# Half of one weight ahead in float32, input tiles of 128 rows, more half output tiles: an attention and soft-MoE kernel on one core

## The chip, the core and the metric

The kernel runs on one core of a Trainium2 chip. TensorE (PE; PEld is its weight load), VectorE (DVE), ScalarE (ACT), GpSimd (POOL) and SyncE (SP) run side by side, and 16 DMA engines move data between HBM and the core's on-chip memory. POOL and SP issue the DMAs; a DMA that POOL issues can cast float32 to bf16 on the way, one that SP issues here copies as it is. The metric is device time in microseconds, the median of several runs.

## The reference

Attention comes first. There are 4 batches, 8 heads, 768 positions and a head dimension of 64. Heads 0, 2 and 6 see all earlier positions; the other five see the first 4 positions and a window of 64. The output is laid out as x, 3072 rows of 512. Then comes a soft mixture of experts with 32 slots, 4 for each of 8 experts:

```python
logits = x @ phi                              # phi: 512 x 32
d = softmax(logits, axis=0)                   # over the 3072 tokens
slot_input = (d.T @ x).reshape(8, 4, 512)
for e in range(8):
    slot_out[e] = relu(slot_input[e] @ w1[e]) @ w2[e]   # w1: 512 x 1024, w2: 1024 x 512
c = softmax(logits, axis=1)                   # over the 32 slots
out = c @ slot_out.reshape(32, 512)           # 3072 x 512
```

The inputs q, k, v are 18.9 MB in float32, w1 and w2 together 33.6 MB; the output is 6.3 MB.

## The kernel before

**A planner sets the order.** `Plan` (L33) holds operations with a name, the engines that may run them, a modelled duration, a due time (`key`), dependencies and buffers. `run` (L69) places them one after the other on a model of the engines and returns the order in which they are emitted; each engine then works through its own instructions in that order. `SHIFTS` (L167) is a table of numbers, one for each operation before the last phase: each moves a due time and may fix a copy to ACT or DVE.

**Loads.** POOL issues all loads of q, k, v and nearly all of the weights, with the cast to bf16, in one fixed order (`dma`, L330). A load is issued only when the eighth before it has landed (L331) and when its buffer is free. There are 11 buffers ("S8"). Batch 0 comes in half tiles (L352), 96 rows each. Batches 1 to 3 come as one tile of 96 partitions for each of q, k and v: 9 loads. The order is batch 0, w0, q1 k1 v1, w1, w2, q2 k2 v2, w3 to w5, q3 k3 v3, w6 to w10. The last weights go into memory that other tensors leave (L862 to L877): w11 to w13 whole, w14 and w15 in halves of 256 output columns, in the order 14 left, 15 left, 14 right, 15 right. (w0 to w7 are w1 of the eight experts, w8 to w15 their w2.)

**The front.** SP issues four DMAs at the start (L460): a quarter of w0 as float32, 4 KB for each of 128 partitions, into memory that is later `expT`; the flags of the heads, repeated for 128 partitions (8 KB in 128 packets); and phi in two DMAs, whose rows are pieces of 32 floats (512 packets). The other three quarters of w0 come through POOL's queue with the cast (L394). At 28 us POOL casts the float32 quarter in two operations (L525). DVE works out the flags on all partitions (L427), and from them ACT and POOL make head flags (L434) and DVE the masks (L440). PE meanwhile multiplies zeros, in groups ZF and ZG (L490 to L508), as fillers.

**Attention.** Each tile of q, k or v is turned by PE transposes (L577), 16 at a time into one of two PSUM buffers ("TR"), and evacuated by ACT or DVE (L321, L323). For each of 16 pairs of heads (p), five groups of score products (L610, `PGROUPS` at L197) go through ACT's exponential (L679) into `pt`; three DVE multiplications apply masks (L626). The score block of key block 0 and query block 5 is made separately, four pairs at once, in `ptx` (L691 to L711), and needs no mask of the diagonal. Products with v (L740) follow, are normalised on DVE (L761) and turned (L773). At the end of each batch come logits (L790), exponentials, slot sums (L821) and `expT` (L854).

**The experts and the output.** After the last batch: slot inputs (L892), fillers Z (L902), first layer H (L915), relu (L925), transposes (L937), second layer W2 (L953). W2.14.0 and W2.15.0 are the left halves of the last two experts' weights, W2.14.1 and W2.15.1 the right ones. After W2.15.0 PE makes the row sums RW (L980), DVE their reciprocals (L986), and ACT scales the left half of the slot outputs (SO.0, L992). Then come output tiles of 128 rows (OM, L1009; evacuation OE on ACT or DVE, L1017 and L1019). `NL = 3` groups of four tiles are made in halves: the left halves, columns 0 to 255, before W2.15.1, stored by POOL; the right halves after it, stored by SP; the other 12 tiles whole, stored by SP in three DMAs (L1025 to L1047).

```python
    ri_src = bass.AP(tensor=is_retrieval.tensor.reshape([H]).bitcast(I32), offset=0, ap=[[0, P], [1, 2 * H]])
    nc.sync.dma_start(w0f, moe_w1[0].rearrange("(di x) f -> di (x f)", x=4)[:, 0:2 * KB])
    a = pl.op("RW", on("PE", 0.7, 0.27), kt + 24, deps=[eto[b] for b in range(B)] + [o_st, w2o[0]], acq=[rw], emit=emit_rw,
```

Of the kernel before, what the change touches and what calls it, by code (L numbers as in the profile page):

```python
# [16 lines left out]
KB = 512  # L17
# [144 lines left out]
def act(cols, extra=0.0):  # L162
# [4 lines left out]
SHIFTS = [-192, 84, -330, 309, -90, -87, 300, -18, 120, -42, -48, -360, -132, -240, 42, -360, 57, -222, 12,  # L167
# [48 lines left out]
def kernel(  # L216
# [46 lines left out]
    phf = sb.tile([P, 4, NS], F32, name="phf")  # L263
# [9 lines left out]
    ri = sb.tile([P, 2 * H], I32, name="ri")  # L273
# [11 lines left out]
    w0f = expT.rearrange("p a c -> p (a c)")[:, 0:4 * KB].bitcast(F32)  # L285
# [4 lines left out]
    rne = xT.rearrange("p a c -> p (a c)")[:, 1792:1824].bitcast(F32)  # L290
# [39 lines left out]
    def dma(name, nbytes, buf, dst, src, deps=()):  # L330
        if len(chain) >= 8:  # L331
            deps = list(deps) + [chain[-8]]
        iss = pl.op("issue " + name, on("POOL", 0.645, 1.4), -100, deps=list(deps) + [fifo[0]],
                    acq=[buf] if buf else [], lead=1.3, emit=lambda o: nc.gpsimd.dma_start(dst(), src))  # L334
        fifo[0] = iss
        took = nbytes / 425000.0
        chain.append(pl.op("land " + name, {"DMA": (took, took + 1.3 + min(2.1, 0.22 * len(chain)))}, -100, deps=[iss] + chain[-1:], lead=3.4))
        return chain[-1]

    def raw_view(buf, p0, p1):  # L340
# [27 lines left out]
    def w_mem(i):  # L368

        m = late_mem[i]() if i in late_mem else slots[wbuf[i].slot][:, :]  # L370
        if i == 0:
            return m[:, 0:8 * KB].rearrange("p (h x) -> p h x", h=2)
# [726 lines left out]
```

## Time and profile before

| what | value |
|---|---|
| median of 3 runs | 150.85 us (150.83 to 151.16) |
| the profiled execution | 150.66 us |
| its span, first to last instruction | 148.9 us |
| granted TensorE clock, mean | 0.959 |
| instructions | 5316 |
| HBM read, written | 52.50 MB, 6.29 MB |

The profile's page gives busy times of each engine, the span in 40 slices with the share and the pace of the DMA engines, and the chain of work that ended last. The views of stretches give, for a window in microseconds, the busy time of PE, PEld, DVE, ACT and POOL (with the number of instructions in brackets), the granted clock, the mean DMA share and the GB/s written. A timeline row gives start, length, engine, line, operation, output and inputs, count, and in brackets the idle time before it and what ended it. A group row gives busy time and mean ns of one after the first bar, and idle time before it after the second.

### The profile page before, as it was taken

To read this page: it belongs to the slowest core of one execution; us is meant where nothing else is said; L and a number is where in the kernel's file an instruction comes from. 1 tells how busy PE (TensorE), PEld (TensorE's weight loads), DVE (VectorE), ACT (ScalarE), POOL (GpSimd) and SP (SyncE) were. 2 spreads that over 40 slices of the span, in tenths; PEclk is the share of its full clock that TensorE was granted. 3 is DMA by queue.
4 is the path that set the end of the run, shared out by engine and by line. 5 is a ranking of instruction groups with operands and counts; after the bars stand their busy time and mean duration, and the time that the engine had idled before them with its cause. 6 is when DMAs were issued, how large, how long until landed. Compare 5 with 4: busy or idle time off the path is not lost.

```text
span 148.9 us, 5316 instructions
## 1 busy us (share of the span) xinstructions
PE 124.9 (84%) x2351; PEld 85.2 (57%) x2351; DVE 109.0 (73%) x231; ACT 108.3 (73%) x139; POOL 34.2 (23%) x60
## 2 busy tenths in 40 slices
PE   6759999889999999998999999999959897659100
PEld 1256667568677676676766776756645553433000
DVE  1843699996999899999799999998974311749400
ACT  3134799989999978998799999999962450638300
POOL 6948411610201200310101104130170000520000
PEclk9999999999999999999999999999999999996855
DMA  5999999999999999999999999999999999999994
GB/s 116 162 209 211 227 205 216 216 214 216 210 217 215 216 216 212 212 218 214 215 214 214 216 214 217 216 212 215 216 215 212 203 198 198 166 328 308 390 425 207
DMA packets 14279, 33.18 MB, mean 223 GB/s; under 512 B 1392, under 2 KB 7024, under 8 KB 13872
## 3 DMA queue, kind: packets, MB, share of 16 engines
q0 software_dynamic: 11408, 27.53, 94.3%
q1 hardware_dynamic: 2848, 5.32, 10.0%
q8 instruction: 18, 0.29, 0.7%
q14 instruction: 5, 0.04, 0.1%
HBM read 52.50 MB, written 6.29 MB: 395 GB/s over the span
## 4 chain that ended last, share of the span: by engine, by line
PE 45%; DMA 20%; DVE 17%; ACT 7%; issue 4%; POOL 1%; DVEq 0%; ACTq 0%; POOLq 0%
DMA qk<-in_moe_w_dram 14%; PE pv L740 12%; PE sc L610 11%; PE tr L577 10%; ACT pt L679 6%; DMA slot<-in_q_dram 5%; DVE xv L761 4%; DVE pt L626 4%; PE bk L1009 3%; PE tr L773 3%; DVE vx L323 2%; PE tr L643 2%; DVE vf L658 2%; PE pv L504 2%; DVE slot L1019 1%
## 5 line engine op out<-in xcount | busy, mean ns | idle before, releaser
L679 ACT ACTIVATE pt<-sc 128x1024 bf16<-128x1024 f32 x80 | 76.8, 1042 | 6.0 <-PE sc L610 5.7
L610 PE MATMUL sc<-qk 64*128 64x128 bf16 (+3 forms) x288 | 32.5, 295 | 1.2 <-ACT pt L679 0.4
L626 DVE TENSOR_TENSOR pt<-pt,msk 128x1024 bf16<-128x1024 bf16 (+1 forms) x48 | 30.7, 658 | 2.1 <-ACT pt L679 1.8
L740 PEld LDWEIGHTS <-pt 128*128 128x128 bf16 x640 | 23.5, 97 | 8.6 <-issue 5.8
L740 PE MATMUL pv<-vx,pt 128*128 128x65 bf16 x352 | 26.3, 193 | 1.1 <-DVE xv L761 0.6
L577 PEld LDWEIGHTS <-slot 96*64 96x64 bf16 x768 | 20.4, 116 | 9.1 <-issue 5.8
L740 PE MATMUL pv<-vf,pt 128*128 128x65 bf16 x288 | 21.6, 194 | 1.0 <-DVE xv L761 0.9
L577 PE MATMUL tr<-ident,slot 96*64 96x96 bf16 x576 | 17.1, 208 | 0.5 <-DVE qk L323 0.5
L610 PEld LDWEIGHTS <-qk 64*128 64x128 bf16 x288 | 11.9, 94 | 8.6 <-issue 2.4
L323 DVE COPY qk<-tr 128x768 bf16<-128x768 bf16 x23 | 12.3, 551 | 6.2 <-PE tr L577 6.2
L761 DVE TENSOR_TENSOR xv<-pv,rs 128x768 bf16<-128x768 f32 (+1 forms) x17 | 15.5, 910 | 0.6
L334 POOL DMA_DIRECT2D slot<-in_moe_w_dram x11 | 7.6, 695 | 31.8 <-PE tr L577 26.7
L321 ACT COPY qk<-tr 128x768 bf16<-128x768 bf16 x9 | 7.2, 810 | 5.8 <-PE tr L577 5.7
L1017 ACT ACTIVATE slot<-bk,rrow 128x256 f32<-128x256 f32 (+1 forms) x17 | 8.1, 553 | 4.2 <-PE bk L1009 4.2
L1019 DVE TENSOR_SCALAR slot<-bk,rrow 128x256 f32<-128x256 f32 (+1 forms) x19 | 9.3, 560 | 0.6 <-PE bk L1009 0.5
L773 PE MATMUL tr<-ident,xv 128*128 128x128 bf16 x96 | 8.4, 220 | 1.3 <-issue 0.5
L577 PE MATMUL tr<-ident_u,slot 96*64 96x96 bf16 x192 | 7.7, 245 | 1.5 <-DMA slot<-in_q_dram 1.5
L323 DVE COPY xv<-tr 128x768 bf16<-128x768 bf16 x15 | 8.0, 552 | 0.8 <-PE tr L577 0.8
L1009 PE MATMUL bk<-msk,expT 128*128 128x256 bf16 (+1 forms) x36 | 7.8, 365 | 0.9 <-DVE msk L994 0.7
L323 DVE COPY vx<-tr 128x768 bf16<-128x768 bf16 x15 | 8.2, 549 | 0.0
L323 DVE COPY xT<-tr 128x768 bf16<-128x768 bf16 (+1 forms) x14 | 7.3, 524 | 1.1 <-PE tr L773 1.0
L643 PE MATMUL tr<-ident,xv 128*128 128x128 bf16 x96 | 8.1, 220 | 0.0
(102 smaller groups left out, 146.8 us busy)
## 6 DMA issues: line engine op xcount, KB each, us to landing
slot<-in_moe_w_dram POOLq DMA_DIRECT2D x10, 1024.0 KB, 25.2
out_dram<-slot SPq DMA_DIRECT2D x3, 1024.0 KB, 6.8
slot<-in_q_dram POOLq DMA_DIRECT2D x3, 768.0 KB, 30.2
slot<-in_k_dram POOLq DMA_DIRECT2D x3, 768.0 KB, 32.0
slot<-in_v_dram POOLq DMA_DIRECT2D x3, 768.0 KB, 22.7
out_dram<-slot SPq DMA_DIRECT2D x3, 512.0 KB, 3.8
qk<-in_moe_w_dram POOLq DMA_DIRECT2D x1, 1024.0 KB, 19.2
vx<-in_moe_w_dram POOLq DMA_DIRECT2D x1, 1024.0 KB, 22.2
```

Source lines behind the costliest of these rows:

```text
L323: nc.vector.tensor_copy(dst, src)
L577: nc.tensor.transpose(dst_, rv[:, i, 8 * c + s, :], idv)
L610: nc.tensor.matmul(scb[sc.slot][:, i, c:c + 128 * nb], kk, qq.rearrange("p b c -> p (b c)"), start=True, stop=True)
L626: nc.vector.tensor_tensor(pT, pT, mh, op=ALU.mult)
L643: nc.tensor.transpose(t[:, 128 * j:128 * (j + 1)], vT[:, 6 * n + j, :], ident)
L679: nc.scalar.activation(pTs[PTb[b, n].slot][:, :, 512 * g:512 * (g + 1)], scb[sc.slot], ACT.Exp, scale=scale)
L740: nc.tensor.matmul(pvb[:, h, 65 * i:65 * (i + 1)], lt, rhs, start=(j == 0), stop=(j == i))
L761: nc.vector.tensor_tensor(xo, pvw[:, :, :, 0:64], r.rearrange("p i (j o) -> p i j o", o=1).to_broadcast([P, 2, i1 - i0, 64]), op=ALU.mult)
L773: nc.tensor.transpose(t[:, 128 * i:128 * (i + 1)], xv[:, i, 128 * n:128 * (n + 1)], ident)
L1009: nc.tensor.matmul(banks[bf.slot][:, 0:w], out_lhs(gi, r), slot_out[:, cs], start=True, stop=True)
L1017: nc.scalar.activation(d, banks[bf.slot][:, 0:w], ACT.Copy, scale=sc_)
L1019: nc.vector.tensor_scalar(d, banks[bf.slot][:, 0:w], sc_, None, op0=ALU.mult)
```

## The change

- **w0**: SP brings half of it, 8 KB for each partition, as float32 into the memory of the second q/k buffer (`qk_mem[1]`), which batch 1 uses. POOL's load of w0 shrinks to the other half, 1 MB in HBM. POOL casts in four operations with due times 8 to 17 us; the evacuations of q and k of batch 1 wait for them.
- **Phi**: one DMA of 128 rows of 512 bytes, then a cast, four transposes, a copy, four transposes and a copy bring it into its layout. **Flags**: one packet to one partition; DVE, a PE product with ones, and DVE spread them.
- **Tiles**: q, k, v of batches 1 to 3 become seven tiles (six of 128 partitions, one of 96), loaded in 13 parts; one evacuation for each part. The loads' order is w0, tiles 0 and 1, w1, tile 2, w2, tiles 3 and 4, w3 to w5, tiles 5 and 6, w6 on.
- **Score groups**: block (0, 5) goes into the last group and block (1, 5) into the fourth; (5, 5) goes into `ptx` and gets a mask of its own, MX. The last group's mask covers 256 columns of each head instead of 384.
- **Fillers**: four ZG groups instead of eight; Z has 10 products of 448 columns instead of 17 of 256.
- **The end**: RW has an earlier due time and no longer waits for W2. `NL = 14` counts tiles: 14 in halves, 10 whole. The first right store is split in two.
- `SHIFTS` is a new table, and the planner's model lets the first load start at 4.6 instead of 3.4.

```diff
 PGROUPS = [
     [(0, 0, 4)],
     [(1, 1, 4)],
     [(2, 2, 4)],
-    [(3, 3, 3), (0, 4, 1)],
-    [(4, 4, 2), (5, 5, 1), (1, 5, 1)],
+    [(3, 3, 3), (1, 5, 1)],
+    [(4, 4, 2), (0, 4, 2)],
 ]
+TILES = [
+    [("q", 1, 0, 24), ("k", 1, 0, 8)],
+    [("k", 1, 8, 24), ("v", 1, 0, 16)],
+    [("v", 1, 16, 24), ("q", 2, 0, 24)],
+    [("k", 2, 0, 24), ("v", 2, 0, 8)],
+    [("v", 2, 8, 24), ("q", 3, 0, 16)],
+    [("q", 3, 16, 24), ("k", 3, 0, 24)],
+    [("v", 3, 0, 24)],
+]
+TKEYS = [10.8, 16.0, 31.0, 36.0, 50.0, 60.5, 68.4]
...
-    w0f = expT.rearrange("p a c -> p (a c)")[:, 0:4 * KB].bitcast(F32)
+    w0f = qk_mem[1][:, 0:8 * KB].bitcast(F32)
...
-    ri_src = bass.AP(tensor=is_retrieval.tensor.reshape([H]).bitcast(I32), offset=0, ap=[[0, P], [1, 2 * H]])
+    ri_src = bass.AP(tensor=is_retrieval.tensor.reshape([H]).bitcast(I32), offset=0, ap=[[2 * H, 1], [1, 2 * H]])
 
     def sp_front(o):
-        nc.sync.dma_start(w0f, moe_w1[0].rearrange("(di x) f -> di (x f)", x=4)[:, 0:2 * KB])
+        nc.sync.dma_start(w0f, moe_w1[0].rearrange("(di h x) f -> h di (x f)", h=2, x=2)[0])
         nc.sync.dma_start(ri, ri_src)
-        pv_ = moe_phi.rearrange("(i n d) s -> i d n s", i=2, n=4)
-        for i in range(2):
-            nc.sync.dma_start(phf[64 * i:64 * (i + 1)], pv_[i])
+        nc.sync.dma_start(phf, moe_phi.rearrange("(p a) s -> p (a s)", a=4))
...
-    for x in range(8):
+    for x in range(4):
         o_z = pl.op(f"ZG{x}", pe(52, 4), 105.0, deps=[o_z], lead=7.8 + 0.7 * x, emit=emit_zg, mode="full", mm=4)
...
-    o_fl = pl.op("flags", on("DVE", 1.55), -10, deps=[o_sp, o_kp], lead=7.0, emit=flags)
+    flb = Buf("TR")
+    o_fr = pl.op("flag row", on("DVE", 0.2), -10, deps=[o_sp], emit=flag_row)
+    o_fp = pl.op("flag product", on("PE", 0.07, 0.27), -10, deps=[o_fr, o_tab], acq=[flb], mode="r32", mm=1,
+                 emit=lambda o: nc.tensor.matmul(trb[flb.slot][:, 0:H], unit[:, 0:128], frow, start=True, stop=True))
+    o_fl = pl.op("flags", on("DVE", 0.45), -10, deps=[o_fp, o_kp], rel=[flb], emit=flags)
...
-    o_phi = pl.op("phi", on("DVE", 0.15), T * 1.5, deps=[o_sp], lead=15.0, emit=lambda o: nc.vector.tensor_copy(phi, phf))
+    o_p = pl.op("phi cast", on("DVE", 0.2), T * 2.0, deps=[o_sp], lead=7.0, emit=lambda o: nc.vector.tensor_copy(phw, phf))
+    o_p = pl.op("phi T1", pe(56, 4), T * 2.1, deps=[o_p, o_id], acq=[pb1], emit=phi_t1, mode="c32", mm=4)
+    o_p = pl.op("phi E1", copy_engs(512), T * 2.2, deps=[o_p], rel=[pb1], emit=phi_e1)
+    o_p = pl.op("phi T2", pe(40, 4), T * 2.3, deps=[o_p], acq=[pb2], emit=phi_t2, mode="r32", mm=4)
+    o_phi = pl.op("phi E2", on("DVE", 0.15), T * 2.4, deps=[o_p], rel=[pb2],
+                  emit=lambda o: nc.vector.tensor_copy(phw, tr_bf(pb2.slot, 4 * NS)))
...
-    o_w0 = [pl.op(f"w0 cast {x}", on("POOL", 1.2), 27.0, deps=[o_sp, wland[0]], lead=26.5 + 1.5 * x,
+    o_w0 = [pl.op(f"w0 cast {x}", on("POOL", 1.2), 8.0 + 3 * x, deps=[o_sp, wland[0].deps[0]], lead=8.0 + 2 * x,
...
+    def tile_transposes(ti):
+        parts = TILES[ti]
+        R = 4 * sum(x1 - x0 for _, _, x0, x1 in parts)
...
+                for s in range(8):
+                    for i in range(2):
+                        nc.tensor.transpose(t[64 * i:64 * (i + 1), :, s, :], rv[:, i, 8 * c + s, :], ident[0:R, 0:R])
...
+            for x, b, x0, x1 in parts:
+                def emit_e(o, c=c, tr=tr, x=x, b=b, x0=x0, x1=x1, y0=y0):
+                    copy(o, dst_of(x, b)()[:, x0:x1, 32 * c:32 * (c + 1)],
+                         tr_bf(tr.slot, 8 * R).rearrange("p (x y) -> p x y", y=32)[:, y0:y0 + x1 - x0, :])
...
+            def emit_mx(o, b=b, ns=ns):
+                px = ptx[PTXb[b].slot][:, :, ns[0]:ns[-1] + 1, :]
+                mh = msk.rearrange("p (i n) c -> p i n c", i=2)[:, :, ns[0]:ns[-1] + 1, 256:384]
+                nc.vector.tensor_tensor(px, px, mh, op=ALU.mult)
...
-    a = pl.op("RW", on("PE", 0.7, 0.27), kt + 24, deps=[eto[b] for b in range(B)] + [o_st, w2o[0]], acq=[rw], emit=emit_rw,
+    a = pl.op("RW", on("PE", 0.7, 0.27), kt + 14, deps=[eto[b] for b in range(B)] + [o_st], acq=[rw], emit=emit_rw,
...
-    NL = 3
...
+    NL = 14
+    halved = [(gi, min(4, NL - 4 * gi)) for gi in range((NL + 3) // 4)]
...
+        for r0, r1 in [(0, 2), (2, 4)] if gi == 0 else [(0, n)]:
+            store("SP", "r", gi, r0, r1, slice(256, 512), kt + 41 + gi + 0.1 * r0)
```

More of the change, by code (lines that the diff above doesn't have):

```diff
@@ L336, in dma @@
         took = nbytes / 425000.0
-        chain.append(pl.op("land " + name, {"DMA": (took, took + 1.3 + min(2.1, 0.22 * len(chain)))}, -100, deps=[iss] + chain[-1:], lead=3.4))
+        chain.append(pl.op("land " + name, {"DMA": (took, took + 1.3 + min(2.1, 0.22 * len(chain)))}, -100, deps=[iss] + chain[-1:], lead=4.6))
         return chain[-1]
@@ L528, with phi_t1, phi_e1, phi_t2 @@
-    batch_loads(1)
+    pb1, pb2 = Buf("TR"), Buf("TR")
+    phw = phi.rearrange("p n s -> p (n s)")
+    def phi_t1(o):
+        t = tr_bf(pb1.slot, DM)[0:NS]
+        for a in range(4):
+            nc.tensor.transpose(t[:, P * a:P * (a + 1)], phw[:, NS * a:NS * (a + 1)], ident)
+    def phi_e1(o):
+        copy(o, t1.rearrange("s (n i y a) -> s n i y a", n=4, i=2, a=4),
+             tr_bf(pb1.slot, DM)[0:NS].rearrange("s (a i n y) -> s n i y a", a=4, i=2, n=4))
+    def phi_t2(o):
+        for n in range(4):
+            nc.tensor.transpose(tr_bf(pb2.slot, 4 * NS)[:, NS * n:NS * (n + 1)], t1[:, 128 * n:128 * (n + 1)],
+                                ident[0:NS, 0:NS])
@@ L529 @@
+    load_tile(0)
+    load_tile(1)
     load_w(1)
+    load_tile(2)
     load_w(2)
-    batch_loads(2)
+    load_tile(3)
+    load_tile(4)
     for i in (3, 4, 5):
         load_w(i)
-    batch_loads(3)
+    load_tile(5)
+    load_tile(6)
     for i in range(6, 11):
@@ L549, in dst_of, with transposes @@
         return {"q": lambda: qTs[QTb[b].slot], "k": lambda: kTs[KTb[b].slot], "v": lambda: vT}[x]
-    def transposes(x, b):
-        raw = raws[x, b]
-        tb = {"q": QTb, "k": KTb, "v": VTb}[x][b]
-        dst = dst_of(x, b)
-        first = True
-        for part in ((0, 1) if b == 0 else (None,)):
+    def transposes(x):
+        raw, tb, dst, first = raws[x, 0], {"q": QTb, "k": KTb, "v": VTb}[x][0], dst_of(x, 0), True
+        for part in (0, 1):
             es = []
-            for c in range(2 if b == 0 else 4):
+            for c in range(2):
@@ L593, in transposes @@
-                es.append(pl.op(f"E{x}{b}.{part or 0}.{c}", copy_engs(768), key, deps=[a], rel=[tr], emit=emit_e))
-                first = False
-            if b == 0:
-                ev[x, 0, part] = es
-            else:
-                ev[x, b] = es
+                            nc.tensor.transpose(t[64 * i:64 * (i + 1), :, :, s, :], rv[:, i, 8 * c + s, :], ident_u)
+                a = pl.op(f"T{x}0.{part}.{c}", pe(23, 16), key, deps=[lands[x, 0, part], o_iu, tb.op],
+                          acq=[tr] + ([tb] if first else []), rel=[raw], emit=emit_t, mode="c64", mm=16)
@@ L600, in evs @@
     def evs(x, b, n):
-        return ev[x, 0, n // 2] if b == 0 else ev[x, b]
+        return ev[x, 0, n // 2] if b == 0 else [e for x0, x1, e in ev[x, b] if x0 < 6 * n + 6 and x1 > 6 * n]
     def sc_mms(sc, b, parts):
@@ L624, in f @@
             else:
-                pT, mh = pT[:, :, 2048:2432], mh[:, :, 256:640]
+                pT, mh = pT[:, :, 2048:2304], mh[:, :, 256:512]
             nc.vector.tensor_tensor(pT, pT, mh, op=ALU.mult)
         return f
-    for b in range(B):
-        for x in "qkv":
-            transposes(x, b)
+    for x in "qkv":
+        transposes(x)
+    for ti in range(len(TILES)):
+        tile_transposes(ti)
     for b in range(B):
```

139 lines of the change are left out of this document (72 added, 67 removed), and 57 rows, old and new, of the table SHIFTS.

## The prediction

> **What bounds the kernel now.** I read the slices of the page first, then the stretches, then the chain of work that ended last, then the timeline of the end.
>
> ```profile
> PE 124.9 (84%) x2351; PEld 85.2 (57%) x2351; DVE 109.0 (73%) x231; ACT 108.3 (73%) x139; POOL 34.2 (23%) x60
> ...
> DMA  5999999999999999999999999999999999999994
> GB/s 116 162 209 211 227 205 216 216 214 216 210 217 215 216 216 212 212 218 214 215 214 214 216 214 217 216 212 215 216 215 212 203 198 198 166 328 308 390 425 207
> ```
>
> No compute engine fills the span, but the DMA line is full from the second slice to the last but one. GB/s counts written bytes: a load that casts float32 to bf16 writes half of what it reads, so 215 here and 425 at the end (float32 stores) are the same pace.
>
> ```profile
> 0.00:2.00 2.00, 0.85 (x3) 0.41 (x4) 0.24 (x1) 1.27 (x1) 0.88 (x5) 1.00 0.06 14
> 2.00:4.00 2.00, 1.57 (x5) 0.33 (x3) 0.76 (x1) 0.01 (x1) 1.92 (x6) 1.00 1.00 223
> 4.00:6.00 2.00, 1.46 (x5) 0.56 (x6) 1.50 (x12) 0.59 (x2) 2.00 (x7) 1.00 0.92 135
> 6.00:8.00 2.00, 1.49 (x4) 0.30 (x2) 1.83 (x7) 0.00 (x0) 2.00 (x5) 1.00 1.15 202
> ...
> 50.00:60.00 10.00, 9.52 (x234) 7.20 (x227) 9.41 (x19) 8.69 (x11) 0.50 (x1) 1.00 1.06 215
> ```
> ```profile
> 20.00:31.00 11.00, 10.27 (x202) 7.26 (x201) 10.60 (x23) 10.85 (x12) 3.61 (x5) 1.00 1.06 214
> ```
> ```profile
> 20.00:108.00 88.00, 84.33 (x1818) 61.60 (x1815) 81.40 (x159) 83.94 (x98) 15.01 (x21) 1.00 1.06 214
> ```
>
> The columns are PE, PEld, DVE, ACT and POOL busy time, then clock, DMA share and GB/s. From 20 us on the loads run at 214, whatever the engines do. Only the front falls short. Beside the loads PE, DVE and ACT are busy 84.3, 81.4 and 83.9 of 88 us: a second bound, close behind.
>
> ```profile
> 109.84 21.38 DMA qk<-in_moe_w_dram
> 131.26 0.42 PE bk L953 x8
> ```
> ```profile
> 125.87 0.40 PE L953 MATMUL bk<-qk,xT 128*32 128x256 bf16 x8 [0.86 <-DMA qk<-in_moe_w_dram]
> ...
> 126.20 0.75 PE L980 MATMUL bk<-cols,expT 128*128 128x1 bf16 x24
> 126.32 0.47 ACT L992 ACTIVATE msk<-bk,rcs 128x256 bf16<-128x256 f32 x1 [4.13 <-PE bk L953]
> ...
> 126.85 0.93 PE L1009 MATMUL bk<-msk,expT 128*128 128x256 bf16 x7
> 126.99 0.31 DVE L986 RECIPROCAL rrow<-bk 128x24 f32<-128x24 f32 x1 [3.31 <-PE bk L980]
> 127.39 2.30 ACT L1017 ACTIVATE slot<-bk,rrow 128x256 f32<-128x256 f32 x6 [0.59 <-PE bk L1009]
> ...
> 132.32 5.80 PE L1009 MATMUL bk<-msk,expT 128*128 128x256 bf16 x24 [0.66 <-DVE msk L994]
> 132.72 6.85 DVE L1019 TENSOR_SCALAR slot<-bk,rrow 128x256 f32<-128x256 f32 x13 [0.45 <-PE bk L1009]
> ```
> ```profile
> 131.50:134.50 3.00, 2.34 (x22) 1.48 (x15) 2.27 (x6) 1.75 (x5) 0.00 (x0) 0.80 0.99 341
> 134.50:135.00 0.50, 0.50 (x3) 0.22 (x2) 0.50 (x2) 0.49 (x2) 0.00 (x0) 0.50 0.26 82
> 135.00:139.00 4.00, 3.12 (x11) 1.02 (x9) 4.00 (x8) 3.47 (x6) 0.00 (x0) 0.78 1.00 340
> 140.00:147.00 7.00, 0.00 (x0) 0.00 (x0) 0.00 (x0) 0.00 (x0) 0.00 (x0) 0.51 1.00 419
> ```
>
> The last weight is used at 131.26. After that the end is a queue of stores: half tiles at 341 and 340, whole tiles at 419, with one hole at 134.5. The output is 6.29 MB, so the end moves with two things: when the loads let go of the DMA engines, and when the first left half is ready. The second starts at W2.15.0 (125.87), which waits for a load, but only 0.86 us of it.
>
> **The front.** These are the four kinds of transfer that the change touches (queue, KB of one, us from issue to landing).
>
> ```profile
> slot<-in_q_dram POOLq DMA_DIRECT2D x2, 384.0 KB, 8.5
> ...
> expT<-in_moe_w_dram SPq DMA_DIRECT2D x1, 512.0 KB, 4.5
> ...
> phf<-in_moe_phi_dram SPq DMA_DIRECT2D x2, 32.0 KB, 9.1
> ri<-in_is_retrieval_dram SPq DMA_DIRECT2D x1, 8.0 KB, 4.2
> ```
>
> From 0 to 6 us the engines wrote 2 x (14 + 223 + 135) = 744 KB. Of these 524 KB are w0's float32 rows and 8 KB the flags, read once; the other 212 KB are cast, so read as 424. That is 0.96 MB read. At 430 GB/s (2 x 215) from 2.0 us on it would be 1.72 MB: a hole of 0.76 MB, or 1.8 us. SP's w0 rows are there 4.5 us after their issue, POOL's first q only after 8.5. The change puts another 524 KB there and takes it from POOL's w0 load: 524 / 430 = 1.2 us if all of it falls into the hole, 0 if none does. Phi in 128 packets instead of 512 and the flags in one instead of 128 free slots from 6 us on: the row of 6 to 8 lacks 13 GB/s, some 0.1 us, and the row of 4 to 6 lacks more for the same reason in part; I take 0.3. Loads end **1.5 us earlier**, bounds 0.1 to 1.9.
>
> The first q rows go behind more bytes of SP, but ahead of fewer phi packets. If the hole takes SP's rows, they land as now; if not, 1.2 us later. I take 0. The flags now wait for one packet behind w0's rows, then a DVE operation, a PE product and DVE again. Behind them DVE has the head masks and a copy, PE the fillers and the first transposes:
>
> ```profile
> 9.03 1.49 PE L577 MATMUL tr<-ident_u,slot 96*64 96x96 bf16 x32 [1.54 <-DMA slot<-in_q_dram]
> ...
> 12.66 0.85 PE L577 MATMUL tr<-ident_u,slot 96*64 96x96 bf16 x16
> ```
> ```profile
> 13.63 0.56 DVE L323 COPY qk<-tr 128x768 bf16<-128x768 bf16 x1 [4.46 <-PE tr L577]
> ```
>
> PE idles 1.54 us ahead of 9.03, DVE 4.46 us ahead of 13.63: the detour costs nothing unless the flags come over 2 us later. Phi's eight transposes and two copies go into the same slack. Four fewer filler groups could leave PE at its early pace (0.85 us for 16 transposes; 0.53 later) for longer: 0 to 1.3 us for 64 transposes, taken at 0, since the real ones run back to back from 15 us.
>
> ```profile
> 33.31 0.53 PE L577 MATMUL tr<-ident,slot 96*64 96x96 bf16 x16 [0.45 <-DVE qk L323]
> ```
>
> **Casts of w0 on POOL.** There are four instead of two, at 8 to 16 us instead of 28. On POOL the loads of the first tiles and the flag copies queue behind them. POOL has by then issued seven loads, 5.8 MB, which is 13 us of the stream from 5 us on, so a delay of some 4 us starves nothing.
>
> ```profile
> 27.97 1.81 POOL L526 CAST slot<-expT 128x512 bf16<-128x512 f32 x2
> ```
> ```profile
> 27.42 0.82 DVE L658 TENSOR_TENSOR vf<-vx,fmx 128x528 bf16<-128x528 bf16 x1
> ```
> ```profile
> 48.70 0.43 DVE L658 TENSOR_TENSOR vf<-vx,fmx 128x528 bf16<-128x528 bf16 x1
> ```
>
> Beside the cast, the same DVE product took 0.82 instead of 0.43 us. Two more contacts at 0.39 are 0.8 us of DVE, but in its slack of the front: 0, up to 0.8. The Trainium skill, "SBUF — State Buffer", § Who interferes with whom, says that a VectorE instruction with two SBUF inputs and a GpSimd instruction that reads SBUF exclude each other for the whole instruction. By it a contact may cost a whole cast; the trace agrees that there is a price, at less than half of that.
>
> **Tiles of 128 rows.** Nine loads of 96 rows become thirteen parts of seven tiles. The stretch of 20 to 31 us is q1, k1 and v1 in 96 rows at 214; 50 to 60 is weights in 128 rows at 215. So the shape gains nothing on the DMA. The Trainium skill's SBUF page, § Summary: rules for kernel authors, would have 128 partitions for a DMA-bound transfer; by it 96 rows might run at three quarters, 161, and the nine loads (14.2 MB read, 33 us at 430) would win 11 us. The trace excludes that. At most eight loads are in flight; any eight in a row of the new ones still read over 7 MB, 17 us, so the stream has work.
>
> On the engines:
>
> ```profile
> L626 DVE TENSOR_TENSOR pt<-pt,msk 128x1024 bf16<-128x1024 bf16 x32 | 22.0, 699 | 1.1 <-ACT pt L679 0.8
> ...
> L577 PE MATMUL tr<-ident,slot 96*64 96x96 bf16 x576 | 17.1, 208 | 0.5 <-DVE qk L323 0.5
> ...
> L323 DVE COPY qk<-tr 128x768 bf16<-128x768 bf16 x23 | 12.3, 551 | 6.2 <-PE tr L577 6.2
> ...
> L626 DVE TENSOR_TENSOR pt<-pt,msk 128x768 bf16<-128x768 bf16 x16 | 9.1, 576 | 1.0 <-ACT pt L679 1.0
> ...
> L323 DVE COPY xT<-tr 128x384 bf16<-128x384 bf16 x2 | 0.7, 352 | 0.4 <-PE tr L773 0.4
> ```
>
> Transposes fall from 576 to 448, each a third longer: equal columns, 128 weight loads fewer, perhaps 1 us of PE. Evacuations rise from 36 to 52 for the same columns. Two copies (768 in 551 ns, 384 in 352) give 153 ns for each extra one: 16 x 0.153 = 2.4 us on DVE and ACT together. The third mask shrinks from 768 to 512 elements: 699 - 576 = 123 ns for 256 elements, 16 times, 2.0 us saved. The new mask of the last diagonal block costs 0.7 for three batches and two halves for the first, some 2.9. Together +3.3 us on two engines, 1.6 us of each, against 4 to 7 us of idle time that each has in 88. The score groups lose a part (six products instead of four now), 32 products of PE. A new table of shifts orders all this anew; no row prices an order, and ACT's 4.1 us of idle bound it both ways. I take the end of compute as **unmoved**, bounds -1 to +2.5.
>
> **The end.** The row sums (0.75 us of PE at 126.20) move ahead. The left product at 126.85 waited for ACT's slot sums (126.79) anyway, but its evacuation began 0.54 later, where on the right side 0.40 is enough: -0.15 (0 to -0.5). Two more left tiles and the split first right store fill the hole at 134.5: (341 - 82) x 0.5 / 341 = 0.38, I take -0.35. Halves go at 340 instead of 419: two tiles are 0.52 MB, 1.54 instead of 1.25 us, +0.3. Loads that end before the left stores begin collide less with them: -0.1.
>
> **Sum.** W2.15.0 comes 0.86 us earlier, no more, since PE is then the later one (loads alone would give 1.5). -0.86 - 0.15 - 0.35 + 0.3 - 0.1 = -1.16. The profiled execution took 150.66 us around its span of 148.9, so 149.5; the median of the runs is 150.85, 0.19 above, so **149.7**.
>
> **Rivals.**
>
> *Compute comes earlier too.* PE loses 128 weight loads and 32 products, and the order is new. With compute 1 us earlier W2.15.0 is bounded by the loads: -1.5 instead of -0.86, so 149.0; with the whole hole filled 148.6. For it: all three engines are busy 93 to 96%, so each saved operation may count. Against: DVE and ACT get more work.
>
> *The hole isn't free.* SP's rows ran at 223 GB/s or less, not 430; the extra ones would hold the same engines until 7 us. First q lands 1.2 us later, compute with it, loads gain 0.5: W2.15.0 at +0.34, the end at about 0, 150.9. This is also the case in which the change doesn't do what it says. For it: the DMA share is 1.00 and 0.92 from 2 to 6 us, so the engines held packets nearly all the time, though they moved little. Against: 223 in the first of these rows and 135 in the second say that w0's rows were mostly through by 4 us, and what came then was slow for a want of packets.
>
> *Slower: the evacuations and the masks.* If neither ACT nor DVE absorbs its 1.6 us, and the split copies hold the two transpose buffers longer, compute ends 2 to 2.5 us later. It decides from 1.16 us on, where W2.15.0's loss eats the rest: at 2.2 us the end is 1.04 later, 151.9. For it: ACT is busy 83.9 of 88. Against: PE gets lighter, and the idle time is larger than the price.
>
> *The casts hold DVE.* Whole casts, by the trace's 0.91 us each, twice more: compute 1.8 later, 151.5 at worst, 151.0 in between. Against: DVE idles there.
>
> **Chances.** Forecast 149.1 to 150.3: 40%. Compute earlier (148.4 to 149.1): 20%. Hole not free (150.3 to 151.2): 14%. Evacuations (151.3 to 152.3): 21%. Casts (150.5 to 151.5): 5%. A measurement here tells about 0.3%, 0.45 us, from no change: below 150.4 is faster, 61%; between, 16%; above 151.3, 23%. The range 148.5 to 151.6 leaves out the slowest half of the evacuations and the tail of early compute.
>
> **What would show it.** Front: the stretch of 4 to 6 us rises well above 135 and the last weight is used before 130.5; if it is still used at 131, the front term is wrong. Compute: W2.15.0 waits for the load hardly at all, or not; if it comes after 125.9 without a wait, compute slipped. End: no hole before the right stores, the left evacuations start 0.4 us behind their products. The forecast is wrong if first q is transposed a microsecond later, or if ACT and DVE gain over 2 us of work between 20 and 108.

## The result, and the profile after

The kernel after takes 148.83 us (median of 6 runs, 148.66 to 150.48), the kernel before in the same comparison 151.36 (6 runs, 150.83 to 151.97). The ratio is 0.9858, with a 95% interval from 0.9813 to 0.9903: 1.0 to 1.9% faster, by the middle 2.1 us. The forecast was 149.7 with a range of 148.5 to 151.6; the time lies in the range and close to a rival, "compute comes earlier too" (149.0, or 148.6 with the whole hole filled).

The profiled execution of after is the longest of its six: 150.48 us, span 148.7. So beside it I read a second one of the same kernel, `a_same` below: 149.34 us, span 147.6, against 150.66 and 148.9 before. Executions over 1.5% longer than the fastest of their kernel count in the medians but not in the ratios, and the profiled execution of `b_long`, below, is one of them, so none of its rows is read. The slices of the page and the first stretches of after:

```profile
DMA  5999999999999999999999999999999999789994
GB/s 134 276 206 210 220 213 212 214 212 214 217 216 215 212 213 214 214 215 219 213 212 213 215 214 223 212 213 212 216 217 214 198 200 195 121 313 339 378 426 205
```
```profile
0.00:2.00 2.00, 0.85 (x3) 0.41 (x4) 0.24 (x1) 1.27 (x1) 0.87 (x5) 1.00 0.27 41
2.00:4.00 2.00, 1.57 (x5) 0.33 (x3) 0.61 (x1) 0.10 (x2) 1.94 (x6) 1.00 0.81 266
4.00:6.00 2.00, 1.53 (x5) 0.56 (x6) 1.33 (x11) 0.51 (x2) 2.00 (x8) 1.00 0.98 307
6.00:8.00 2.00, 1.58 (x5) 0.40 (x3) 1.79 (x8) 0.00 (x0) 2.00 (x4) 1.00 1.14 209
```

The stretch of 4 to 6 us went from 135 to 307 GB/s: the front is filled. Behind it the pace is the same 214. The slice at 128 us has sunk from 166 to 121, a first hint that in this execution something other than the loads was late. The two timelines of the end (start, length, engine, line, operation, idle time and its releaser), after first:

```profile
104.55 6.53 ACT L735 ACTIVATE pt<-sc 128x1024 bf16<-128x1024 f32 x7
...
126.26 0.39 PE L1017 MATMUL bk<-pt,xT 128*32 128x256 bf16 x8
126.47 0.39 PE L1017 MATMUL bk<-qk,xT 128*32 128x256 bf16 x8
127.44 2.29 PE L1073 MATMUL bk<-msk,expT 128*128 128x256 bf16 x14 [0.58 <-ACT msk L1056]
...
130.15 0.40 PE L1017 MATMUL bk<-qk,xT 128*32 128x256 bf16 x8
```
```profile
104.30 3.82 ACT L735 ACTIVATE pt<-sc 128x1024 bf16<-128x1024 f32 x4
...
124.10 0.40 PE L1017 MATMUL bk<-qk,xT 128*32 128x256 bf16 x8 [0.39 <-DMA qk<-in_moe_w_dram]
125.08 2.29 PE L1073 MATMUL bk<-msk,expT 128*128 128x256 bf16 x14 [0.57 <-ACT msk L1056]
...
130.85 0.62 PE L1017 MATMUL bk<-qk,xT 128*32 128x256 bf16 x8 [3.15 <-DMA qk<-in_moe_w_dram]
```

In the second, PE was ready for W2.15.0 at 123.71 (124.10 less the 0.39 of waiting), before at 125.01: compute came 1.3 us earlier in this pair of executions. The load was there at 124.10 instead of 125.87: loads came 1.8 earlier. Both moved, so the left half moved by 1.77, not by 0.86. In the long execution compute was late instead (126.47, without a wait), and it differs from the second at its start:

```profile
24.51 0.85 PE L613 MATMUL tr<-ident_u,slot 96*64 96x96 bf16 x16
26.96 0.53 PE L613 MATMUL tr<-ident_u,slot 96*64 96x96 bf16 x16
```
```profile
17.40 0.81 PE L613 MATMUL tr<-ident_u,slot 96*64 96x96 bf16 x16
19.66 0.53 PE L613 MATMUL tr<-ident_u,slot 96*64 96x96 bf16 x16
```

PE kept its slow early pace until 25 to 27 us in the first, until 17 to 20 in the second; before, it turned between 15.32 (32 in 1.49) and 17.58 (32 in 0.87). The two are the same code, so the turn varies between executions, and it goes with the 1.1 us that lie between them. The other profiled executions with this order of work (`a_quarter`, `a_tailold`, `a_fill8` and `a_packets`, below) fall in line: where the pace had turned by 18 us the last exponential ended at 107.7 to 108.1, where it turned at 21 at 109.0 and 109.2, and in the long one at 111.1.

The end of the second, by stretches:

```profile
128.00:131.00 3.00, 0.15 (x4) 0.14 (x7) 0.61 (x2) 0.00 (x0) 1.79 (x3) 0.94 1.04 346
131.00:133.00 2.00, 1.34 (x13) 0.62 (x6) 0.92 (x3) 0.22 (x1) 0.00 (x0) 0.50 1.03 371
133.00:134.50 1.50, 1.50 (x9) 1.06 (x8) 1.50 (x5) 1.33 (x4) 0.00 (x0) 0.50 0.28 104
134.50:138.00 3.50, 3.50 (x12) 1.51 (x11) 3.07 (x7) 2.69 (x6) 0.00 (x0) 0.57 0.99 344
```

The hole ahead of the right stores, which the two more left tiles were to fill, is back: 104 GB/s from 133 to 134.5. The left stores moved forward with W2.15.0, while W2.15.1 could start only at 130.85, 0.41 before its old 131.26. The trace's completions of that last weight (one from each of 16 shares) came by 129.38 for fifteen shares and at 130.81 for the last.

### The profile page after: what moved, and what is told of

Its sections match the earlier page's. It is cut to its first block, busy times and chain, and to the rows that moved or that the text cites. A ratio compares the mean times of both kernels' runs of the same rounds, so it can differ in the third digit from the quotient of the medians.

```text
span 148.7 us, 5009 instructions
## 1 busy us (share of the span) xinstructions
PE 125.0 (84%) x2179; PEld 83.4 (56%) x2179; DVE 110.0 (74%) x252; ACT 107.4 (72%) x144; POOL 37.8 (25%) x67
## 4 chain that ended last, share of the span: by engine, by line
PE 40%; DVE 24%; ACT 19%; DMA 5%; issue 4%; DVEq 0%; ACTq 0%; POOLq 0%
ACT pt L735 14%; PE sc L665 8%; PE pv L804 7%; PE tr L613 6%; DMA slot<-in_q_dram 5%; DVE pt L681 5%; DVE qk L335 4%; DVE slot L1083 4%; DVE xv L825 4%; PE tr L639 3%; ACT qk L333 3%; PE bk L979 2%; PE tr L699 2%; PE bk L1017 2%; PE bk L1073 2%
## 5 line engine op out<-in xcount | busy, mean ns | idle before, releaser
L665 PE MATMUL sc<-qk 64*128 64x512 bf16 (+3 forms) x256 | 32.8, 323 | 2.8 <-ACT pt L735 1.9
L681 DVE TENSOR_TENSOR pt<-pt,msk 128x1024 bf16<-128x1024 bf16 (+1 forms) x48 | 28.4, 596 | 1.6 <-ACT pt L735 1.4
L665 PEld LDWEIGHTS <-qk 64*128 64x128 bf16 x256 | 10.7, 95 | 10.2 <-issue 3.8
L639 PE MATMUL tr<-ident,slot 128*64 128x128 bf16 (+1 forms) x448 | 15.7, 219 | 0.0
L639 PEld LDWEIGHTS <-slot 128*64 128x64 bf16 (+1 forms) x448 | 12.8, 110 | 4.3 <-issue 4.2
L335 DVE COPY qk<-tr 128x768 bf16<-128x768 bf16 (+2 forms) x28 | 12.6, 463 | 2.8 <-PE tr L613 1.7
L333 ACT COPY qk<-tr 128x768 bf16<-128x768 bf16 (+2 forms) x12 | 8.4, 698 | 8.6 <-PE tr L613 7.9
L335 DVE COPY xv<-tr 128x768 bf16<-128x768 bf16 (+2 forms) x19 | 8.4, 445 | 2.5 <-PE tr L613 2.0
L613 PE MATMUL tr<-ident_u,slot 96*64 96x96 bf16 x192 | 9.1, 270 | 1.3 <-DMA slot<-in_q_dram 1.3
L613 PEld LDWEIGHTS <-slot 96*64 96x64 bf16 x192 | 7.4, 155 | 4.4 <-issue 2.8
```

Source lines behind the costliest of these rows:

```text
L333: nc.scalar.copy(dst, src)
L335: nc.vector.tensor_copy(dst, src)
L613: nc.tensor.transpose(t[64 * i:64 * (i + 1), :, :, s, :], rv[:, i, 8 * c + s, :], ident_u)
L639: nc.tensor.transpose(t[64 * i:64 * (i + 1), :, s, :], rv[:, i, 8 * c + s, :], ident[0:R, 0:R])
L665: nc.tensor.matmul(scb[sc.slot][:, i, c:c + 128 * nb], kk, qq.rearrange("p b c -> p (b c)"), start=True, stop=True)
L681: nc.vector.tensor_tensor(pT, pT, mh, op=ALU.mult)
```

## The experiments

My theory: the front's hole sets the end of the loads, and the end follows as far as compute lets it. The rivals: the gain comes from compute (the tiles and their new order); or from the end alone. Three comparisons, each on one chip with its own runs of before: medians 151.21 (17 runs), 151.10 (30) and 151.60 (23). Ratios are against these.

### The kernel after again, and with less or more of one part

**a_same**: no edit.

> The changed kernel again, to see which of its executions is the usual one. In the profiled execution (150.48 us) PE keeps its slow early pace, 0.85 us for 16 transposes, until about 26 us; the five others took 148.66 to 148.86. Theory: the pace of PE at the front decides; a profile of an execution near 148.8 shows 0.53 us for 16 transposes well before 26 us and ends its last exponential about 1.5 us earlier than the 111.1 of the slow one. Rival: the early pace is the same in both, and the 1.7 us come from the end or from the DMAs.

148.98 (6 runs), ratio 0.9858 (0.9818 to 0.9899): the same ratio as in the first comparison. Its rows stand above. The pace turned near 18 us, as the theory has it, and the last exponential ended at 108.12 instead of 111.08, twice the gain expected. The time fell by only 1.1, since W2.15.1 then waited 3.15 us for its load; so the pace isn't all of it.

**a_quarter**: the early float32 part is a quarter of w0 again; phi, flags, tiles and end as in after. The order on every engine is unchanged; POOL's four casts cover half as much.

```diff
-nc.sync.dma_start(w0f, moe_w1[0].rearrange("(di h x) f -> h di (x f)", h=2, x=2)[0])
+nc.sync.dma_start(w0f[:, 0:2 * KB], moe_w1[0].rearrange("(di x) f -> di (x f)", x=4)[:, 0:2 * KB])
...
```

> The changed kernel with only a quarter of w0 in front as float32 (4 KB rows) and three quarters by POOL, as before; the order of every engine but the numbers of POOL's casts stays. Theory that the loads are the bound and the front's hole is real: loads end about 1.2 us later, and the kernel takes 0.8 to 1.2 us longer than the changed one, 149.6 to 150.0. Rival that the hole isn't free or that compute is the bound by now: 0 to 0.3 us longer.

150.45 (12 runs), ratio 0.9939 (0.9908 to 0.9970): the quarter more in front is worth 0.8%, 1.2 us on 151.2 (1.5 by the medians). In its stretches:

```profile
4.00:6.00 2.00, 1.53 (x5) 0.56 (x6) 1.33 (x11) 0.51 (x2) 2.00 (x8) 1.00 0.82 154
6.00:8.00 2.00, 1.58 (x5) 0.39 (x3) 1.76 (x8) 0.00 (x0) 2.00 (x4) 1.00 1.05 187
```
```profile
132.26 0.62 PE L1019 MATMUL bk<-qk,xT 128*32 128x256 bf16 x8 [3.13 <-DMA qk<-in_moe_w_dram]
```

154 instead of 307: the hole is there again. The last data packet of the loads came at 130.46, in `a_same` at 129.03: 1.4 later, near the 1.2 that 524 KB take at 430 GB/s. W2.15.0 came without a wait here (125.54), but W2.15.1 waited for its load until 132.26, 1.4 later than in `a_same`. So the last load sets the end, and the rows in the hole are needed.

**a_tailold**: after with the old end (12 half tiles, first right store whole, row sums late).

```diff
-    a = pl.op("RW", ..., kt + 14, deps=[eto[b] for b in range(B)] + [o_st], acq=[rw], ...
+    a = pl.op("RW", ..., kt + 24, deps=[eto[b] for b in range(B)] + [o_st, w2o[0]], acq=[rw], ...
...
-    NL = 14
+    NL = 3
...
```

> The changed kernel with the end of before: 12 tiles in halves, one first right store, row sums after W2. Theory: the end is worth about 0.3 us (0.15 for the row sums, 0.35 for the hole, less 0.3 for the shorter rows, 0.1 for fewer collisions), so 149.1. Rival that the half tiles are the main gain: 0.8 us or more, over 149.6. Rival that the short rows eat it all: 148.8 or less.

149.24 (5 runs), ratio 0.9865 (0.9835 to 0.9896). The new end gives 0.3 us by the medians, as forecast, but the intervals overlap.

**a_fill8**: after with eight instead of four filler products in each ZG group.

```diff
-        for _ in range(4):
+        for _ in range(8):
             nc.tensor.matmul(pvb[:, 0, 392:512], zt[:, 0:128], ...
```

> The changed kernel with eight products in each of its four filler groups instead of four, so as many filler products as before. Theory that the halved fillers let PE stay at its slow early pace in some executions: none at 150.5 any more, all near 148.7, and 16 transposes take 0.53 us by 20 us. Rival that the fillers don't matter: slow executions as often as in the changed kernel. If PE is on the path at the front, the longer groups themselves cost some 0.3 us.

148.70 (4 runs, 148.56 to 148.97), ratio 0.9834 (0.9801 to 0.9867). All four runs lie near 148.7, as the theory has it, but so do eight of the twelve of after and `a_same`, and the interval overlaps that of after: it is not shown to be faster. Of all kernels run it has the lowest median.

### The parts alone, on the kernel before

**b_front**: half of w0 early in float32 rows of 8 KB, cast by POOL from 8 us on; phi, flags, tiles and end as before. PE, DVE and ACT work in the order of before.

```diff
-nc.sync.dma_start(w0f, moe_w1[0].rearrange("(di x) f -> di (x f)", x=4)[:, 0:2 * KB])
+nc.sync.dma_start(w0f, moe_w1[0].rearrange("(di h x) f -> h di (x f)", h=2, x=2)[0])
...
```

> The kernel before, with the half of the first weight in float32 rows put in front and nothing else changed; tiles, flags, phi and the end are as before. Theory A (the front hole sets the end): the loads end about 1.3 us earlier and the time falls by as much as the end of compute allows; in the trace of before the weight of the third last product group was waited for by only 0.86 us, so 150.0 to 150.5 us against 151.2, with the last weight's data complete before 130.0. Rival B (the gain of the whole change comes from compute): 151.0 to 151.4, loads earlier and PE later than they are everywhere at the end.

151.72 (12 runs), ratio 1.0053 (1.0032 to 1.0074): slower, which neither theory expected. Its front shows why:

```profile
2.00:4.00 2.00, 1.57 (x5) 0.33 (x3) 0.75 (x1) 0.02 (x1) 1.92 (x6) 1.00 0.80 258
4.00:6.00 2.00, 1.46 (x5) 0.56 (x6) 1.49 (x12) 0.59 (x2) 2.00 (x7) 1.00 0.56 218
6.00:8.00 2.00, 1.50 (x5) 0.30 (x2) 1.42 (x6) 0.00 (x0) 2.00 (x5) 1.00 0.86 143
```
```profile
5.00:6.50 1.50, 1.50 (x5) 0.58 (x5) 1.36 (x10) 0.00 (x0) 1.50 (x5) 1.00 0.23 31
6.50:7.00 0.50, 0.50 (x3) 0.15 (x1) 0.47 (x2) 0.00 (x0) 0.50 (x2) 1.00 0.70 113
7.00:9.00 2.00, 0.50 (x2) 0.00 (x0) 1.41 (x7) 0.00 (x0) 1.54 (x3) 1.00 1.19 212
```

The early rows fill 2 to 5 us, but then the engines stand nearly empty: 31 GB/s and a share of 0.23 from 5 to 6.5. In the trace's packets these are the flags: 128 packets of 64 bytes, started between 4.78 and 7.14, and hardly a load among them: 11 load packets start from 5 to 6.5 us, in the trace of before 120. Phi's 512 packets come after, from 7.00 on, and beside them the loads run at 212. Before, the flags ran from 3.28 to 4.94, beside w0's rows, when the loads had hardly begun. Behind longer rows they come just when the loads should. The last data packet of the loads came at 131.57, 0.7 later than before, and the time rose with it.

**b_tail**: before with the new end alone (the edit of `a_tailold` the other way).

> The kernel before, with the end of the kernel after: 14 half tiles on the left, the first right store in half rows, row sums taken early. My prediction priced this at -0.5 on the bracket (row sums -0.15, hole -0.35) and +0.3 on the half rows, so about -0.3: 150.7 to 151.0. Rival: 0, since the end is set by when the last weight is complete, 151.1 to 151.4.

150.29 (12 runs), ratio 0.9958 (0.9941 to 0.9974): -0.4 to -0.9 us, in the middle twice what I had priced. PE was ready for W2.15.0 at 124.81 (before 125.01) and used the weight at the same time; what moved is behind it:

```profile
125.86 0.40 PE L953 MATMUL bk<-qk,xT 128*32 128x256 bf16 x8 [1.05 <-DMA qk<-in_moe_w_dram]
126.84 2.46 PE L1009 MATMUL bk<-msk,expT 128*128 128x256 bf16 x14 [0.57 <-ACT msk L992]
```

The 14 left products now run without a gap, in 2.46 us; before, twelve took from 126.85 to 129.02.

**b_front_tail**: both.

> The kernel before with both, the early half of the first weight and the new end; tiles of 96 rows, phi and flags as before. What is left to the kernel after are the tiles of 128 rows with their order, phi and the flags. Theory A (those leave the time as it is, as predicted): 148.8 to 149.3. Rival B (the tiles bring compute forward by about 1 us): 149.6 to 150.3. Rival C (the tiles cost, as the evacuations could): below 148.5.

151.05 (12 runs), ratio 1.0011 (0.9988 to 1.0034). It lies beyond what all three theories gave, because all three held the front for a gain. -0.6 of the end and +0.8 of the front make about nothing.

**b_fill2**: before with half as many filler products per ZG group (`range(2)`).

> The kernel before with half as many filler products per group at the start; nothing else is changed. Theory (fewer fillers keep PE at its slow early pace, 0.85 us for 16 transposes, for longer): the pace turns fast later than 19.3 us after the start, and 0.3 to 1.0 us is lost: 151.5 to 152.2. Rival (the early pace has nothing to do with the fillers): 151.0 to 151.4, with the turn at 17 to 19 us as before.

152.78 (7 runs), ratio 1.0083 (1.0052 to 1.0115). Slower, by more than expected, and not by the expected way. The early pace turned between 14.53 (32 in 1.49) and 16.80 (32 in 0.96), no later than before; the time went later, where the granted clock fell:

```profile
20.00:40.00 20.00, 17.69 (x411) 13.22 (x410) 18.00 (x36) 18.43 (x22) 5.18 (x7) 1.00 1.06 214
40.00:60.00 20.00, 19.14 (x365) 14.14 (x365) 15.55 (x31) 15.72 (x19) 1.39 (x2) 0.83 1.06 215
```

0.83 is the clock, and ACT, which has the exponentials, got through 15.72 us of work instead of 18.40. But this is one execution, and the clock fell to half for some 3 us in others too, with the fillers as they were in the kernel concerned (`a_quarter` and `a_tailold` from 110 to 114 us) or doubled (`b_fill8`, from 113 to 116). So whether the fillers have to do with it is open, and my theory on them has no support.

### What the small packets do, and what the tiles leave

**a_packets**: after, with the 128 flag packets and 512 phi packets of before loaded once more, behind the new rows, into memory that nobody reads. Engine orders unchanged.

```diff
+nc.sync.dma_start(spare_r, bass.AP(..., ap=[[0, P], [1, 2 * H]]))
+for i in range(2):
+    nc.sync.dma_start(spare_p[64 * i:64 * (i + 1)], pv_[i])
```

> The kernel after, with the 128 flag packets and the 512 phi packets of before loaded once more, behind the new rows, into memory that nobody reads; the order of PE, DVE, ACT and POOL is unchanged. Theory A (the small packets, not only the missing rows, keep the cast loads from starting): in the stretch of 5 to 6.5 us the loads all but stop, as they do with the early half alone on the kernel before, the last weight is complete about 1.3 us later, and the time is 150.0 to 150.6 against about 148.9. Rival B (the packets are hidden beside the cast loads' start, as I had costed them): 148.8 to 149.2.

150.33 (6 runs), ratio 0.9912 (0.9880 to 0.9945): 0.5%, some 0.8 us, slower than after by the ratios, as theory A has it, though the intervals just overlap. Its front:

```profile
4.00:6.00 2.00, 1.54 (x5) 0.56 (x6) 1.34 (x11) 0.50 (x2) 2.00 (x8) 1.00 1.04 326
6.00:8.00 2.00, 1.58 (x5) 0.40 (x3) 1.76 (x8) 0.00 (x0) 2.00 (x4) 1.00 0.75 96
```

96 instead of 209 with the packets: 2 x 113 = 226 KB less written, 452 read, 1.05 us at 430. The last data came at 130.53, 1.5 later than in `a_same`. W2.15.0 waited 2.23 us for its load, until 125.55 (`a_same`: 124.10); W2.15.1 came at 130.91, hardly later than the 130.85 of `a_same`, where one share was late. Most of the flags' packets started between 5.9 and 8.4 us, which is where the loads crawl: 91 load packets start from 6 to 8 us, in `a_same` 205, and the engines' share is 0.75 instead of 1.12. Phi's packets start from 8.08 on, beside loads at 196 and 218 again. The Trainium skill, "DMA: Bandwidth & Descriptors", § Specifications, asks for at least 512 bytes in one transfer for full pace. By that rule phi's pieces of 128 bytes fall short like the flags, and there are four times as many; in the traces the loads stood beside the flags' 64 bytes alone, all read from one place in HBM. No run here takes the flags and phi apart.

**b_long**: `b_front` with phi in 512-byte rows and the flags in one packet, spread by a product. Phi isn't turned, so its values stand in another order.

```diff
-    nc.sync.dma_start(phf[64 * i:64 * (i + 1)], pv_[i])
+nc.sync.dma_start(phf, moe_phi.rearrange("(p a) s -> p a s", a=4))
...
```

> The kernel before with the early half of the first weight, phi loaded in 512-byte rows and the flags in one packet; the turning of phi is left out, so its values stand in another order and the outputs are wrong; the flags are spread by one small product. Engine orders are those of the early half alone (151.7). Theory A (the small packets behind the rows are what cost that kernel its gain): the stretch of 4 to 8 us carries above 500 GB/s over its two halves, the loads end 1.5 to 2 us earlier than with the half alone, and the time falls to 150.2 to 150.8, then bound by compute. Rival B (it is slower because of the casts or the order): 151.5 to 151.9.

150.11 (6 runs), ratio 0.9902 (0.9865 to 0.9938). From `b_front`'s 1.0053, measured on another chip, that is -1.5%, 2.3 us, for the packets alone. The casts are the same in both, so rival B falls. The time is a little below theory A's. The loads can be seen in `b_long_tail`, which has the same front: the last data came at 129.70, 1.9 before those of `b_front`.

**b_long_tail**: the same with the new end.

> The same with the new end as well; what is left to the kernel after are the tiles of 128 rows, the engine order that goes with them, and phi's two turns; the outputs are wrong in phi here too. Theory A (front rows and packets give 1 us, the end 0.7, the tiles and their order the rest of 2.2): 149.4 to 150.0. Rival B (tiles and order give nothing, as my forecast had it): 148.7 to 149.1. Rival C (the front gives nothing on the kernel before): 150.8 to 151.2.

150.52 (12 runs, 149.33 to 152.12), ratio 0.9921 (0.9886 to 0.9956): no faster than `b_long`, and above theory A's 149.4 to 150.0. After is at 0.9858, so what is left gives another 0.6%, 1 us, more than theory A gave it; the intervals just overlap. What is left is more than the expectation names: the tiles, the new score groups, the fewer fillers, phi's turns and the order of all of it. The front is that of after, and compute isn't:

```profile
4.00:6.00 2.00, 1.48 (x5) 0.56 (x6) 1.50 (x12) 0.59 (x2) 2.00 (x7) 1.00 1.00 318
6.00:8.00 2.00, 1.64 (x5) 0.40 (x3) 1.64 (x7) 0.00 (x0) 2.00 (x5) 1.00 1.11 209
```
```profile
104.13 5.65 ACT L678 ACTIVATE pt<-sc 128x1024 bf16<-128x1024 f32 x6
...
125.68 0.39 PE L952 MATMUL bk<-qk,xT 128*32 128x256 bf16 x8
```

Loads as early as in the long execution of after (last data 129.70, there 129.79), but PE reaches W2.15.0 at 125.68 without a wait. So in this execution, without the new tiles, the left half is bound by compute, and the new end has little to add.

The group of the exponentials separates the two designs in all executions read. Its last figure is the time that ACT idled for score products: before, `b_long_tail`, `b_front`, `b_tail`, then the kernel after, `a_same`, `a_packets`:

```profile
L679 ACT ACTIVATE pt<-sc 128x1024 bf16<-128x1024 f32 x80 | 76.8, 1042 | 6.0 <-PE sc L610 5.7
```
```profile
L678 ACT ACTIVATE pt<-sc 128x1024 bf16<-128x1024 f32 x80 | 76.9, 1046 | 7.0 <-PE sc L609 6.6
```
```profile
L677 ACT ACTIVATE pt<-sc 128x1024 bf16<-128x1024 f32 x80 | 77.1, 1041 | 5.4 <-PE sc L608 5.1
```
```profile
L679 ACT ACTIVATE pt<-sc 128x1024 bf16<-128x1024 f32 x80 | 76.7, 1043 | 6.3 <-PE sc L610 6.0
```
```profile
L735 ACT ACTIVATE pt<-sc 128x1024 bf16<-128x1024 f32 x80 | 77.1, 1054 | 5.0 <-PE sc L665 4.9
```
```profile
L735 ACT ACTIVATE pt<-sc 128x1024 bf16<-128x1024 f32 x80 | 77.0, 1055 | 3.0 <-PE sc L665 3.0
```
```profile
L743 ACT ACTIVATE pt<-sc 128x1024 bf16<-128x1024 f32 x80 | 76.8, 1055 | 1.9 <-PE sc L673 1.9
```

The exponentials cost the same 77 us everywhere. With tiles of 96 rows ACT waits 5.1 to 7.1 us for scores (8.5 in `b_fill2`), with the new ones 1.7 to 3.8, and 4.9 in the long execution. The turn of PE's early pace is not what separates them, since it came by 18 us in all of the former. The time at which PE was ready for W2.15.0 is less clear: 124.8 to 127.7 in six executions with tiles of 96 rows (before, `b_tail`, `b_front`, `b_front_tail`, `b_fill8`, `b_long_tail`), 123.3 to 126.5 in six with the new ones. The two groups overlap, 1.5 us apart in the mean.

**b_fill8**: before with eight products per ZG group.

> The kernel before with twice the filler products per group at the start. Theory (more fillers end PE's slow early pace sooner, as halving them prolonged it and cost 1.7 us): 150.5 to 151.0, with the pace of 0.53 us for 16 transposes from 17 us on or earlier. Rival (before's fillers are enough, only fewer hurt): 151.0 to 151.3.

151.58 (12 runs), ratio 0.9988 (0.9967 to 1.0009): no gain. Though the slow pace ended earlier (16 transposes in 0.60 us at 13.45), the time stayed. The rival holds: before's fillers were enough. (That halving them had prolonged the pace, as the theory says, the turn in `b_fill2` doesn't bear out.)

## Why the prediction was right, and where it was not

- **The front, loads 1.5 us earlier.** Right in sum: 135 became 307, and the last data came 1.84 earlier in `a_same` (130.87 to 129.03), 1.1 in the long execution. But the terms inside were mis-sized. I gave the rows 1.2 and the packets 0.3, for phi's and the flags' together. In after the last data come 1.4 later without the extra rows (`a_quarter`) and 1.5 later with the packets (`a_packets`), so each is needed, and the two don't add. The packets, the flags' by the trace, are the condition for the whole: with them left behind the new rows the kernel is 0.5% slower than before (`b_front`), with them gone 1% faster (`b_long`), and put back into after they cost about 0.8 us (`a_packets`). By the sign that I had set, the last weight used before 130.5, the long execution passes (130.15) and `a_same` doesn't (130.85): its data were there, but for one late share. My rival "the hole isn't free" was true of `b_front`, but by what follows the rows, not by the rows.
- **First q rows as now.** Right: first transposed at 8.90 and 8.04, before 9.03. In `a_packets` it was 9.32.
- **Flags and phi at nothing.** No wait of PE or DVE for them shows in after; not tested alone.
- **Fewer filler groups at nothing.** Neither shown nor excluded: `a_fill8` overlaps with after, and the varying turn of PE's pace, with which executions of after get longer, was not shown to follow the fillers.
- **Casts of w0 on POOL at nothing.** No cost shows; not tested alone. They took 0.62 to 0.64 us each, not 0.91. Two of DVE's masks beside them took 0.70 and 1.04 us instead of 0.35 and 0.68 (`a_same`), 0.35 more each, near the 0.39 I had priced. DVE was busy 5.5 of the 10 us from 10 to 20.
- **Tiles of 128 rows: the end of compute unmoved.** This step failed. Compute ended 1.3 us earlier in `a_same`, beyond my bound of -1, and 1.3 and 1.7 earlier in `a_fill8` and `a_packets`. It was 0.1 to 1.5 later in `a_tailold`, `a_quarter` and the long execution, whose pace turned late (in the first two the clock also fell to half from 110 to 114 us). The profiled execution nearest to the usual 148.7 of after is that of `a_fill8`, 148.56. I had added up what ACT and DVE do (+1.6 us each; from 20 to 108 us it is +1.1 and +1.7 in `a_same`) and taken their idle time as cover. What counted, by the rows, was what ACT waited for: PE's scores. The wait for them fell from 5.7 to 3.0. I had put PE's part at perhaps 1 us for the transposes and at nothing for the score products. The rows of before and `a_same` have more (the transposes of before, 17.1 us, stand in the prediction):

```profile
L610 PE MATMUL sc<-qk 64*128 64x128 bf16 (+3 forms) x288 | 32.5, 295 | 1.2 <-ACT pt L679 0.4
```
```profile
L665 PE MATMUL sc<-qk 64*128 64x512 bf16 (+3 forms) x256 | 31.7, 313 | 2.7 <-ACT pt L735 1.9
L639 PE MATMUL tr<-ident,slot 128*64 128x128 bf16 (+1 forms) x448 | 15.7, 219 | 0.0
```

  The 448 transposes are not a third longer each: with a mean of 219 ns against 208 they take 1.4 us less. The 256 score products for 288 (in the last two groups four for each head instead of five, not six) take 0.8 less. Which of the two, or the new order, does it wasn't separated: the order was tuned anew together with the tiles.
- **The end, -0.3 net.** Right in sign: -0.6 on before; the -0.3 on after is within the noise. In `a_same` the hole didn't go, it moved to 133 to 134.5 with the last weight's last share. Half rows ran at 337 to 347, as priced.
- **The sum.** W2.15.0 moved by 1.77 instead of 0.86, since both of the things that bound it moved. W2.15.1 gave part back. The forecast of -1.16 became -2.1 by the ratio. The rival at 20% named the size, and its reason, a lighter PE and a new order, fits the rows of PE without being shown alone. That the time lies in the range owes something to the margin: as a change, the range was -2.35 to +0.75 on the 150.85 of before, so the -2.1 lies inside, but the 2.5 between the two medians would not.

## What to carry to other kernels

A hole at the start of the DMA stream can be filled from a second queue, but ask what follows on that queue: with small packets behind the new rows, by the trace the 128 of 64 bytes, the main stream lost more than was won. When two bounds lie within a microsecond, price a change on both, and price compute by what the busiest engine waits for, not by the idle time of the engines that get more work. Measure parts alone and together: here one part alone was slower, and the whole was faster than the sum of the parts tried alone.

## What the runs showed of the hardware that was not expected

- Beside 128 packets of 64 bytes, 8 KB in all, the loads stood at 31 GB/s written for 1.5 us (`b_front`), though the engines showed a share of 0.23; beside 512 packets of 128 bytes, right after, they ran at 212.
- PE's early pace, 0.85 us for 16 transposes against 0.53, ended between 13 and 27 us in executions of nearly the same code, while the clock in the rows stood at 1.00 until then. In two executions of the same kernel it goes with about 1 us. The Trainium skill, "TensorE: Matmul & The Clock Gate", § What's actually happening, has PE at half rate until it has been busy for one window of some 3.4 us, and says that the count varies from run to run. The pace agrees in kind: 16 more transposes in a run add 0.64 us at first (0.85 to 1.49) and 0.34 later (0.53 to 0.87), nearly half. A slow phase until 27 us is longer than that rule gives.
- The last share of the last weight completed 1.4 us behind the other fifteen in `a_same`, when the last data packet of the loads had long gone (129.03). In that time the trace has a 16 KB instruction transfer (0.97 us from 128.79) and the left stores on the same engines. In `a_quarter` the same stands 1.4 later (transfer at 130.20, PE's wait until 132.26); in `a_fill8`, with the transfer at 126.27, the share was 0.9 us late. The stores behind it have one late completion too, by 1.1 to 1.2 us in `a_same` and 0.9 in `a_fill8`. In `a_packets` the transfer came at 129.90, when the last weight was all but complete: its last share is 0.03 late, those of the stores behind it 0.7 to 0.8. That fits one engine that falls behind by about a transfer. But in `a_tailold`, with a transfer at 128.55, no share of the last weight is late. The trace doesn't say which engine carried the transfer, and no run moved it on purpose, so the cause stays open.
